# Last twenty attention steps as ten blocks of two steps with two dense groups at once, and a quotient by reciprocal on VectorE

## The chip, the cores and the metric

One core of one Trainium2 chip runs the program. The metric is device time in microseconds (us), the median of repeated executions. TensorE (PE) multiplies matrices into PSUM, which has eight banks of 128 x 512 f32; its weight loads (PEld) run beside its multiplications. ScalarE (ACT) applies functions, VectorE (DVE) and GpSimd (POOL) do elementwise work, SyncE (SP) issues the transfers. Each engine works through its own list of instructions in order.

## The reference

```python
def _A_ref(x, wq, wk, wv, wo):          # 32 heads of 16, one shared k and v
    scores = einsum("bhqd,bkd->bhqk", q, k) * (Dh ** -0.5)
    p = softmax(scores)
    return (p @ v) @ wo
def _B_ref(x, w1, b1, w2):
    h = x @ w1 + b1
    act = h * tanh(softplus(h))          # Mish
    return act @ w2
xn = layernorm(x)                        # x is 2048 x 512
s = _A_ref(xn, wq, wk, wv, wo)
g = silu(_B_ref(xn, w1, b1, w2))         # y / (1 + exp(-y))
return x + s * g
```

## The kernel before

The 2048 rows are taken in four chunks of 512 (`NC`). A unit is four heads of one chunk; there are 32 units of 16 steps, 512 steps in all (`NS`). One step takes 128 keys: four score products (`e`, L1025), each 128 keys by 512 rows for one head, an exponential of each on ACT from PSUM into an SBUF tile (`pts` or `pt`, L1030), and two steps later four value products (`pv`, L1112) that add them into one bank. The two score products of a pair stand on the two row halves of the PE array: a score needs 64 of its 128 rows, and even and odd ones alternate.

Beside the attention run the dense products in groups (`Group`): the projections, the two layers of the gate (`xps`) and the output projection (`wop`). A group adds 9 to 15 products of three-term split f32 into one bank (`Mm`). A full product uses all 128 rows (`Mm.__call__`, L112); `Mm.half` (L116) uses 64 rows and needs a second half later on the other side. Up to step 489 dense groups run as halves, on the side that the scores leave free, together with row maxima (`m`, L1054) that DVE reduces (L1058). The maxima of all units are done `LEAD` = 22 steps ahead of the end, so the last 22 steps, 490 to 511, have scores, exponentials, value products and what is left of the dense work.

These last steps are written out in the loop from L1543 on. Steps 490 and 491, and 504 to 511, are single: four scores, up to four full dense products (`fill(4)`), four value products. Steps 492 to 503 are six blocks of two steps: six scores, up to eight full dense products of one group (`fill(8)`), ACT jobs, two scores, eight value products. Scores of these steps take banks from two pools of three, `ps_e` and `ps_m` (L1015); a score waits until the exponential that read the bank before has ended.

The second gate layer of the last chunk leaves one sum `y` (128 x 512) for each of four row tiles `tt`. Its third group adds its product to `y` on DVE (L847); `s1` takes exp(-y) on ACT and limits it on POOL (L855, L179), `s2` takes Ln(e + 1) (L860), `s3` Exp of minus that (L865) and POOL multiplies (L169): y / (1 + exp(-y)). In the same way `n0` and `n1` (L1136, L1140) take the softmax sum of unit 30 to its reciprocal in `sc`, and `n2` makes the output tile `ot_all` on POOL. ACT jobs stand in a queue that the loop empties at marked places (`act_jobs`).

The output projection of the last chunk is split (`wo_groups`): nine of twelve products of each row tile run before the last unit ends, each in a bank of its own (`alloc`), the last three after it. The first group of tiles 0, 1, 2, 3 may start from step 496, 504, 507 and 512 on.

Of the kernel before, what the change touches and what calls it, by code (L numbers as in the profile page):

```python
# [39 lines left out]
HALF = P // 2  # L40
HOLD = 1
STEP_US = 2.88
K_US = {0: 2.7, 6: 2.86, 7: 3.07, 8: 3.07}
UNIT_US = 11.75
XMAX = 8
NPT = 14
# [76 lines left out]
def block_kernel(ctx: ExitStack, tc: tile.TileContext, x, wq, wk, wv, wo, w1, b1, w2, out):  # L123
# [53 lines left out]
    def pool_min(o, lim):  # L177
        charge(0.7)
        pool.tensor_scalar(o, o, lim, 0.0, op0=ALU.min, op1=ALU.max)  # L179
# [216 lines left out]
    def later(k, fn):  # L396
        at(step[0] + k, fn)
# [3 lines left out]
    def job(fn, free=None):  # L401

        jobs.append((fn, free))
# [184 lines left out]
    def chunk_size(n):  # L588
        return -(-n // -(-n // XMAX)) if n else 0
# [238 lines left out]
    def m2_groups(c, third, its, m1s):  # L828
        lo, hi = THIRDS[third]

        def ready(tt):
            done = m1_done.get((c, hi - 1))
            return None if done is None else done - g_of[tt].most

        g_of = []

        def mk(tt):
            def post(ps):
                if tt == 3:
# [7 lines left out]
                dve.tensor_tensor(out=y, in0=ps, in1=y, op=ALU.add)  # L847
                if third < 2:
                    return
                st = {}  # L850

                def s1():
                    e = st["e"] = sb.tile([P, D], F32, tag="t", name=f"e{c}_{tt}", bufs=2)
                    st["free"] = hold(t_hist)
                    act.activation(e, y, AF.Exp, scale=-1.0)  # L855
                    pool_min(e, EMAX)
                    at(pool_at(0.3), lambda: job(s2))

                def s2():
                    act.activation(st["e"], st["e"], AF.Ln, bias=one)  # L860
                    job(s3)

                def s3():
                    e = st["e"]
                    act.activation(e, e, AF.Exp, scale=-1.0)  # L865
                    mul(pool, y, y, e)
                    y_done[c, tt] = pool_at(0.2)
                    st["free"]()
                later(0.5, lambda: job(s1, t_free))

            g = Group(mm12(lambda j, a: act_of[c, lo + j][:, a, P * tt:P * (tt + 1)],
                           lambda j, b: its[j].tile[:, b], hi - lo), post, its, [lambda: ready(tt)])
            g.dve = third > 0
            g.late = 3 if hi - lo == 5 else 2
            g_of.append(g)
            return g
        return [mk(tt) for tt in range(4)]
# [6 lines left out]
    def wo_groups(c):  # L884
        last = c == NC - 1
        its = [item("wb", ("o", k), wo[P * k:P * (k + 1), :]) for k in range(4)]
        first, second = [], []
        adds = []

        def mk(tt):  # L890
            st = {}
            t = 4 * c + tt

            def pre():
                if xr_hist[-4] is None:
                    return False
                st["x"] = sb.tile([P, D], F32, tag="xr", name=f"xr{t}", bufs=4)
                st["free"] = hold(xr_hist)
                sp_at(0.5)
                sp.dma_start(st["x"], xr[t])  # L900
                return True

            def store():
                sp.dma_start(outr[t], st["x"])
                st["free"]()

            def post(ps):
# [12 lines left out]
                at(step[0] if last else pool_at(0.1), store)  # L920

            mms = mm12(lambda j, a: ot_of[c, j][:, a, P * tt:P * (tt + 1)],
                       lambda j, b: its[j].tile[:, b], 4)
            done = [lambda: ot_done.get((c, 3)), lambda: y_done.get((c, tt))]
            if not last:
                first.append(Group(mms, post, its, done, pre, wo=c))
                first[-1].dve = True
                return
            kept = {}

            def alloc():
                pool_, tag = ((ps_x, "x"), (ps_m, "m"), (ps_m, "m"), (ps_e, "e"))[tt]
                kept["ps"] = pool_.tile([P, D], F32, tag=tag, name=f"wop{tt}")
                return kept["ps"]
            first.append(Group(mms[:9], lambda ps: None, its, [lambda: NS - (16, 8, 5, 0)[tt], lambda: ot_done.get((c, 2))], wo=c, alloc=alloc))
# [72 lines left out]
    def e_one(s, i):  # L1008

        v, r = divmod(s, 16)  # L1010
        if s < NS - LEAD:
            a, k, p = 1 - s % 2, r - r % 2 + i // 2, i % 2
        else:
            a, k, p = i % 2, r, i // 2
        ps, tag = (ps_m, "m") if NS - LEAD <= s and i in ((1, 3) if s < NS - 8 else (3,)) else (ps_e, "e")  # L1015
        pt = None
        if i > 1 and s % 4 == 1 and PAIRS[0] < s < PAIRS[1]:
            pt = sb.tile([P, C], F32, tag=("qh", "ql")[i - 2], name=f"pt{s}_{i}", bufs=1)
        return score(v, a, k, p, ps, tag, pt)()

# [93 lines left out]
    def o_out(v):  # L1114
        c, g = divmod(v, 8)
        b, k = divmod(g, 2)
        os_ = sb.tile([P, C], F32, tag="os", name=f"os{v}", bufs=1)
        if v == NU - 1:
            o_last(os_)
            return  # L1120
        act.activation(os_, pv_of[v], AF.Copy)
        if k == 0:
            o_of[0] = sb.tile([P, C], F32, tag="oc", name=f"oc{v}", bufs=1)
            o_of[1] = sb.tile([P, C], F32, tag="sc", name=f"sc{v}", bufs=1)
        oc, sc = o_of[0], o_of[1]
        for e, t in ((16, sc), (0, oc)):
            for j in range(4):
                r = 64 * k + 16 * j
                sp_at(0.63)
                sp.dma_start(t[r:r + 16], os_[32 * j + e:32 * j + e + 16])  # L1130
        rows = slice(0, HALF if v == NU - 2 else P)
        if v == NU - 2:
            turn_rows()
        if k == 1 or v == NU - 2:
            def n0():
                act.activation(sc[rows], sc[rows], AF.Ln)  # L1136
                job(n1)

            def n1():
                act.activation(sc[rows], sc[rows], AF.Exp, scale=-1.0)  # L1140
                later(0.5, n2)

            def n2():
                if b == 0 and c > 0 and wo_left[c - 1]:
                    later(0.5, n2)
                    return
                ot = ot_of[c, b] = ot_all[:, b]
                mul(pool, oc[rows], oc[rows], sc[rows])
                hi_pool(ot[rows, 0], oc[rows])
                sub(pool, ot[rows, 1], oc[rows], f(ot[rows, 0]))  # L1150
                if k == 1:
                    ot_done[c, b] = pool_at(0.2)
            later(3, lambda: job(n0))

    turn_of = {}

# [335 lines left out]
    def unit_ready(s):  # L1492
# [7 lines left out]
            g.most = 2  # L1500
        return ok and 12 < len(cur["g"].mms) <= len(UNIT) - 1

    for s in range(NS + 2000):
        inm = s < NS - LEAD
        if s < skip[0]:
# [87 lines left out]
```

## Time and profile before

| | |
|---|---|
| median of 3 runs | 1575.98 us (1575.85 to 1577.67) |
| the profiled execution, its time | 1576.23 us |
| the profiled execution, span of its instructions | 1574.5 us |
| PE busy over the span | 1559.7 us, 99% |
| ACT, DVE, POOL busy | 1295.0, 1333.2, 636.8 us |
| scores of step 490 start | 1503.09 us |
| scores of step 510 start | 1555.57 us |
| last value product ends, output projection's last products follow | 1561.43 us |

Times inside the profile are counted from the span's start. The busy shares are averages over the whole span; the change touches the last 72 us alone, where DVE has next to nothing to do. A PE instruction's time in the profile overlaps its neighbours' on the other row half or column group, so lengths of stretches are read from start to start.

### The profile page before, as it was taken

How to read it: one execution, taken by the hardware profiler on the slowest of the kernel's cores; microseconds unless marked ns; L12 is line 12 of the kernel's file. 1: busy time of each engine (PE TensorE's matmuls, PEld its weight loads, DVE VectorE, ACT ScalarE, POOL GpSimd, SP SyncE). 2: the span in 40 equal slices, each digit the busy share in tenths (PEclk: the TensorE clock that was granted, in tenths of full speed). 3: DMA queues.
4: the chain of work that ended last, by engine and by line, in shares of the span. 5: the costliest groups of instructions: out<-in, count | busy, mean ns of one | idle time of the engine just before them, and what ended most of it. 6: DMA issues, size and time to landing. Idle time of an engine off the chain costs nothing.

```text
span 1574.5 us, 31330 instructions
## 1 busy us (share of the span) xinstructions
PE 1559.7 (99%) x11681; PEld 876.0 (56%) x11681; DVE 1333.2 (85%) x2275; ACT 1295.0 (82%) x2509; POOL 636.8 (40%) x672
## 2 busy tenths in 40 slices
PE   9999999999999999999999999999999999999998
PEld 6555655655555565565555556556555555655643
DVE  7998888888989988888898988888889898888821
ACT  6489888789898778977989788897888978888796
POOL 4787348356356203321615422162153423215021
PEclk9999999999999999999999999999999999999999
DMA  6243134133141303212123230322322213031200
GB/s 206 88 138 105 46 97 149 32 112 118 45 157 51 106 16 111 72 32 93 50 69 98 91 92 21 103 64 83 97 58 78 76 46 113 15 98 32 75 21 27
DMA packets 74119, 125.21 MB, mean 80 GB/s; under 512 B 21536, under 2 KB 35648, under 8 KB 73968
## 3 DMA queue, kind: packets, MB, share of 16 engines
q1 hardware_dynamic: 73968, 123.21, 25.2%
q8 instruction: 93, 1.52, 0.4%
q14 instruction: 58, 0.48, 0.1%
HBM read 75.31 MB, written 26.21 MB: 64 GB/s over the span
## 4 chain that ended last, share of the span: by engine, by line
PE 96%; ACT 2%; DVE 1%; DMA 0%; POOL 0%; issue 0%; DVEq 0%; POOLq 0%; ACTq 0%
PE xps L116 43%; PE pv L1112 31%; PE m L1054 11%; PE e L1025 6%; PE xps L112 2%; ACT pts L1030 1%; DVE mb L1058 1%; PE warm L1269 1%; PE kp L335 0%; PE wop L112 0%; PE xp L294 0%; PE warm L1348 0%; DMA rawwb<-in_dram 0%; DMA ks<-ks 0%; ACT hb L778 0%
## 5 line engine op out<-in xcount | busy, mean ns | idle before, releaser
L1058 DVE TENSOR_REDUCE mb<-m 128x1 f32<-128x512 f32 x2048 | 1265.7, 682 | 169.6 <-PE m L1054 121.6
L1030 ACT ACTIVATE pts<-e 128x512 f32<-128x512 f32 x2042 | 1062.8, 607 | 220.6 <-PE e L1025 157.1
L1054 PE MATMUL m<-ks,qt 48*128 48x512 f32 (+1 forms) x2048 | 841.5, 425 | 1.2 <-DMA ks<-ks 0.7
L1025 PE MATMUL e<-qt,ks 64*128 64x512 f32 x2048 | 748.0, 407 | 1.8 <-ACT pts L1030 1.7
L1112 PE MATMUL pv<-pts,vaug 128*32 128x512 f32 x4084 | 531.0, 603 | 0.0
L1054 PEld LDWEIGHTS m<-ks,qt 48*128 48x128 f32 (+1 forms) x2048 | 367.3, 185 | 106.7 <-DVE mb L1058 53.2
L1025 PEld LDWEIGHTS e<-qt,ks 64*128 64x128 f32 x2048 | 372.3, 186 | 28.6 <-ACT pts L1030 19.1
L116 PE MATMUL xps<-wbs,act 64*128 64x512 f32 x1248 | 315.2, 397 | 0.0
L116 PE MATMUL xps<-xt,ws 64*128 64x512 f32 x1128 | 313.3, 410 | 0.3 <-ACT pts L1030 0.3
L116 PEld LDWEIGHTS xps<-xt,ws 64*128 64x128 f32 x1128 | 194.5, 185 | 183.4 <-ACT pts L1030 121.4
L116 PEld LDWEIGHTS xps<-wbs,act 64*128 64x128 f32 x1248 | 225.9, 185 | 66.4 <-ACT pts L1030 32.7
L1112 PEld LDWEIGHTS pv<-pts,vaug 128*32 128x32 f32 x4084 | 87.8, 108 | 151.1 <-issue 143.1
L169 POOL TENSOR_TENSOR hb<-hb,t 128x512 f32<-128x512 f32 x56 | 72.2, 1289 | 161.6 <-ACT t L797 81.3
L179 POOL TENSOR_SCALAR t<-t 128x512 f32<-128x512 f32 x56 | 34.4, 614 | 180.1 <-ACT t L784 180.0
L116 PE MATMUL xps<-xt,wq 64*128 64x512 f32 x336 | 93.0, 409 | 0.0
L116 PEld LDWEIGHTS xps<-xt,wq 64*128 64x128 f32 x336 | 57.9, 185 | 55.2 <-ACT pts L1030 37.7
L116 PE MATMUL xps<-wbs,ot_all 64*128 64x512 f32 x288 | 79.3, 408 | 0.0
L169 POOL TENSOR_TENSOR oc<-oc,sc 128x512 f32<-128x512 f32 (+1 forms) x16 | 20.6, 1290 | 144.8 <-DMA wbs<-w 71.3
L116 PEld LDWEIGHTS xps<-wbs,ot_all 64*128 64x128 f32 x288 | 49.5, 184 | 46.9 <-ACT pts L1030 28.5
L169 POOL TENSOR_TENSOR act<-hb,act 128x512 fp32r<-128x512 f32 x56 | 72.2, 1289 | 4.7
L169 POOL TENSOR_TENSOR hb<-hb,u 128x512 f32<-128x512 f32 x56 | 72.2, 1290 | 4.4
L169 POOL TENSOR_TENSOR u<-u,t 128x512 f32<-128x512 f32 x56 | 71.9, 1284 | 4.7
(146 smaller groups left out, 872.0 us busy)
## 6 DMA issues: line engine op xcount, KB each, us to landing
wbs<-w SPq DMA_DIRECT2D x38, 512.0 KB
ws<-w SPq DMA_DIRECT2D x35, 512.0 KB
qt<-qh SPq DMA_DIRECT2D x256, 32.0 KB
w<-wbs SPq DMA_DIRECT2D x14, 512.0 KB
wq<-wq SPq DMA_DIRECT2D x14, 512.0 KB
wbs<-wo SPq DMA_DIRECT2D x12, 512.0 KB
w<-ws SPq DMA_DIRECT2D x11, 512.0 KB
rawws<-in_dram SPq DMA_DIRECT2D x21, 256.0 KB
```

Of the source, the lines that this page charges most:

```text
L112: self.pe.matmul(ps, self.lhs(), self.rhs(), start=(self.k == 0), stop=(self.k == self.tot - 1))
L116: i = self.pe.matmul(ps, self.lhs()[o], self.rhs()[o], start=(self.k == 0 and self.halves == 0), stop=(self.k == self.tot - 1 and self.hal ...
L169: eng.tensor_tensor(out=o, in0=a, in1=b, op=op)
L179: pool.tensor_scalar(o, o, lim, 0.0, op0=ALU.min, op1=ALU.max)
L1025: pe.matmul(e, ks[o:o + 64, P * k:P * (k + 1)], q[o:o + 64, p], start=True, stop=True)
L1030: x = act.activation(dst, e, AF.Exp, scale=0.25)
L1054: pe.matmul(m, q[o, p, P * t:P * (t + 1)], ks[o, C * kb:C * (kb + 1)], start=True, stop=True)
L1058: return dve.reduce_max(out=mb_of[v][:, kb, z:z + 1], in_=m, axis=AX.X)
L1112: pe.matmul(o[32 * j:32 * j + 32], vaug[:, k], pt, start=(k == 0), stop=(k == 15))
L1269: pe.matmul(warm, qts[0][:, 0, 0:P], qts[0][:, 0], start=True, stop=True)
```

## The change

The region of two-step blocks now reaches from step 490 to step 509: ten blocks (`PAIRS`). A block (`tail_block`) issues the four scores of its first step, then the dense work, then the four scores of its second step, then eight value products. Its dense work comes from two groups at once (`lanes`): a chunk of up to eight products of each, as halves, one group on row half 0 and the other on row half 1, issued in turn. In the next block the same two chunks run again on the other halves. The third group of row tile 2 takes a bank of `ps_m` (`y2ps`), and all of the first three output groups may start from step 496.

For row tiles 1 to 3 of the last chunk, `s2` and `s3` are gone: POOL limits e and adds 1, and DVE takes the reciprocal and multiplies. For unit 30, `n_last` takes the reciprocal of `sc` on DVE in place of `n0` and `n1`.

```diff
-K_US = {0: 2.7, 6: 2.86, 7: 3.07, 8: 3.07}
+K_US = {-1: 2.3, 0: 2.7, 6: 2.86, 7: 3.07, 8: 3.07}
...
                     act.activation(e, y, AF.Exp, scale=-1.0)
+                    if c == NC - 1 and tt > 0:
+                        charge(0.7)
+                        pool.tensor_scalar(e, e, EMAX, 1.0, op0=ALU.min, op1=ALU.add)
+                        dve.reciprocal(e, e)
+                        ew(dve, y, y, e, ALU.mult)
+                        y_done[c, tt] = pool_at(0.2) + 2
+                        st["free"]()
+                        return
                     pool_min(e, EMAX)
...
+            if (c, third, tt) == (NC - 1, 2, 2):
+                g.alloc = lambda: ps_m.tile([P, D], F32, tag="m", name="y2ps")
...
-                pool_, tag = ((ps_x, "x"), (ps_m, "m"), (ps_m, "m"), (ps_e, "e"))[tt]
+                pool_, tag = ((ps_m, "m"), (ps_x, "x"), (ps_m, "m"), (ps_e, "e"))[tt]
...
-            first.append(Group(mms[:9], lambda ps: None, its, [lambda: NS - (16, 8, 5, 0)[tt], ...
+            first.append(Group(mms[:9], lambda ps: None, its, [lambda: NS - (16, 16, 16, 0)[tt], ...
...
-        ps, tag = (ps_m, "m") if NS - LEAD <= s and i in ((1, 3) if s < NS - 8 else (3,)) else (ps_e, "e")
+        ps, tag = (ps_m, "m") if NS - LEAD <= s and i in ((1, 3) if s < NS - 6 else (3,)) else (ps_e, "e")
         pt = None
-        if i > 1 and s % 4 == 1 and PAIRS[0] < s < PAIRS[1]:
+        if i > 1 and s % 4 == 3 and PAIRS[0] < s < PAIRS[1]:
...
-            later(3, lambda: job(n0))
+            def n_last():
+                dve.reciprocal(sc[rows], sc[rows])
+                n2()
+            if v == NU - 2:
+                later(4, n_last)
+            else:
+                later(3, lambda: job(n0))
...
-    PAIRS = NS - LEAD + 2, NS - 8
+    PAIRS = NS - LEAD, NS - 2
...
+    def tail_block(s):
...
+            side = (s // 2 + n) % 2
+            mms = ln["g"].mms
+            second = ln["chunk"] is not None
+            if not second:
+                left = len(mms) - ln["n"]
+                ln["chunk"] = mms[ln["n"]:ln["n"] + (left if s >= NS - 6 else chunk_size(left))]
+            for k, m in enumerate(ln["chunk"]):
+                def half(m=m, k=k, ln=ln, side=side, second=second):
+                    i = m.half(ln["ps"], side)
...
+                xs[side].append(half)
...
+        es = [[(s + j // 2, 2 * (j % 2) + a) for a in range(2)] for j in range(4)]
+        for j in range(2):
+            for e in es[j]:
+                e_one(*e)
+        for j in range(max(len(x) for x in xs)):
+            for x in xs:
+                if j < len(x):
+                    x[j]()
+        for ln in ends:
+            for i in ln["g"].items:
+                i.users -= 1
+            ln["g"].post(ln["ps"])
+            ln["g"].done = s
+        relay = e_one(*es[2][0])
+        for e in es[2][1:] + es[3]:
+            e_one(*e)
...
+        act_jobs(3)
+        for n in range(s - 2, s):
+            pv(n)
...
             if s % 2 == 0:
-                es = [(s + n // 4, n % 4) for n in range(8)]
-                for n in es[:6]:
-                    e_one(*n)
-                fill(8)
-                act_jobs(4)
-                for n in es[6:]:
-                    e_one(*n)
-                for n in range(s - 2, s):
-                    pv(n)
-                if s % 16 == 0:
-                    o_out(s // 16 - 1)
+                tail_block(s)
+            halves[0] = -1
```

How the lists of instructions move, at three places. Names: `e_6_0_1` is the score of step 6 of the unit, head pair 0, row half 1; the block of steps 502 and 503 has steps 6 and 7 of unit 31. `wop` are banks of the output projection, the number telling which; `wop_20934` is row tile 0 and `wop_21034` row tile 1 after the change.

PE before, the block of steps 502 and 503: six scores, one full product, two scores, the value products.

```order
L1025 MATMUL e_6_1_1_21017<-qt_78,ks 128x512
L1025 MATMUL e_7_0_0_21020<-qt_78,ks 128x512
L1025 MATMUL e_7_0_1_21023<-qt_78,ks 128x512
L112 MATMUL wop_20975<-wbs,ot_all 128x512
L1025 MATMUL e_7_1_0_21030<-qt_78,ks 128x512
L1025 MATMUL e_7_1_1_21033<-qt_78,ks 128x512
L1112 MATMUL pv_20946<-pts,vaug 32x512 x6
```

PE after, the same block: four scores, nine halves of two output groups, four scores, the value products.

```order
L1035 MATMUL e_6_0_0_21035<-qt_78,ks 128x512
L1035 MATMUL e_6_0_1_21038<-qt_78,ks 128x512
L1035 MATMUL e_6_1_0_21041<-qt_78,ks 128x512
L1035 MATMUL e_6_1_1_21044<-qt_78,ks 128x512
L116 MATMUL wop_20934<-wbs,ot_all 128x512
L116 MATMUL wop_21034<-wbs,ot_all 128x512
```

The second group of the output projection now has its first half here; before, its first full product stood in step 504. Its bank is the one of `ps_x` that row tile 3's third gate group has just left.

The sums of the gate's third group and what DVE holds around them. DVE before, its list from the last row maxima on:

```order
L847 TENSOR_TENSOR y_1_18731<-xps,y_1_18731 128x512
L1087 STREAM_TRANSPOSE cr_20801<-mp_20705 128x32
L847 TENSOR_TENSOR y_2_19039<-xps,y_2_19039 128x512
L847 TENSOR_TENSOR y_3_19200<-xps,y_3_19200 128x512
L1169 COPY os_21200<-pv_20946 128x256
```

DVE after, from the same place:

```order
L1097 STREAM_TRANSPOSE cr_20763<-mp_20705 128x32
L847 TENSOR_TENSOR y_1_18731<-xps,y_1_18731 128x512
L859 RECIPROCAL e_1_20859<-e_1_20859 128x512
L169 TENSOR_TENSOR y_1_18731<-y_1_18731,e_1_20859 128x512
L847 TENSOR_TENSOR y_2_19039<-y2ps,y_2_19039 128x512
L859 RECIPROCAL e_2_20972<-e_2_20972 128x512
L169 TENSOR_TENSOR y_2_19039<-y_2_19039,e_2_20972 128x512
L1164 RECIPROCAL sc_20920<-sc_20920 64x512
L847 TENSOR_TENSOR y_3_19200<-xps,y_3_19200 128x512
L859 RECIPROCAL e_3_21070<-e_3_21070 128x512
L169 TENSOR_TENSOR y_3_19200<-y_3_19200,e_3_21070 128x512
L1185 COPY os_21257<-pv_20977 128x256
```

Four reciprocals and three products came to DVE. The sum that empties `y2ps` (row tile 2) stands behind one reciprocal and one product, and the sum that empties row tile 3's `xps` behind two reciprocals and one product.

ACT before, in the block of steps 494 and 495:

```order
L1030 ACTIVATE pts<-e_15_0_0_20823 128x512
L1030 ACTIVATE pts<-e_15_0_1_20826 128x512
L860 ACTIVATE e_1_20782<-e_1_20782,one 128x512
L865 ACTIVATE e_1_20782<-e_1_20782 128x512
L1030 ACTIVATE pts<-e_15_1_0_20837 128x512
L1030 ACTIVATE pts<-e_15_1_1_20840 128x512
```

ACT after, at the end of the same block:

```order
L1040 ACTIVATE pts<-e_15_0_0_20845 128x512
L1040 ACTIVATE pts<-e_15_0_1_20848 128x512
L1040 ACTIVATE pt_2_20851<-e_15_1_0_20852 128x512
L1040 ACTIVATE pt_3_20855<-e_15_1_1_20856 128x512
L855 ACTIVATE e_1_20859<-y_1_18731 128x512
L1040 ACTIVATE pts<-e_0_0_0_20872 128x512
```

The two instructions between the exponentials of a step are gone for row tiles 1 to 3; what is left of the quotient on ACT stands behind the eighth exponential of a block.

More of the change, by code (lines that the diff above doesn't have):

```diff
@@ L931, in alloc @@
             def alloc():
-                pool_, tag = ((ps_x, "x"), (ps_m, "m"), (ps_m, "m"), (ps_e, "e"))[tt]
+                pool_, tag = ((ps_m, "m"), (ps_x, "x"), (ps_m, "m"), (ps_e, "e"))[tt]
                 kept["ps"] = pool_.tile([P, D], F32, tag=tag, name=f"wop{tt}")
                 return kept["ps"]
-            first.append(Group(mms[:9], lambda ps: None, its, [lambda: NS - (16, 8, 5, 0)[tt], lambda: ot_done.get((c, 2))], wo=c, alloc=alloc))
+            first.append(Group(mms[:9], lambda ps: None, its, [lambda: NS - (16, 16, 16, 0)[tt], lambda: ot_done.get((c, 2))], wo=c, alloc=alloc))
             second.append(Group(mms[9:], post, its, done, pre, wo=c, alloc=lambda: kept["ps"]))
@@ L1501, in unit_ready @@
         return ok and 12 < len(cur["g"].mms) <= len(UNIT) - 1
+    lanes = [None, None]
+    def tail_block(s):
+        if s == PAIRS[0] and cur["g"] is not None:
+            lanes[0] = {"g": cur["g"], "ps": cur["ps"], "n": cur["n"], "chunk": None}
+            cur["g"] = None
+        xs = [[], []]
+        ends = []
+        for n in range(2):
+            if lanes[n] is None and begin():
+                lanes[n] = {"g": cur["g"], "ps": cur["ps"], "n": 0, "chunk": None}
+                cur["g"] = None
+            ln = lanes[n]
+            if ln is None:
+                continue
+            side = (s // 2 + n) % 2
[7 more added lines that the diff above has]
+                    i = m.half(ln["ps"], side)
+                    if second and k == 0:
+                        tc.add_manual_dep(i.ins, ln["relay"].ins.name, mybir.DependencyInfo(
+                            mybir.DependencyClass.Sync, mybir.DependencyReason.DATA), reason="other half of the bank")
+                xs[side].append(half)
+            if second:
+                ln["n"] += len(ln["chunk"])
+                ln["chunk"] = None
+                if ln["n"] == len(mms):
+                    ends.append(ln)
+                    lanes[n] = None
+        es = [[(s + j // 2, 2 * (j % 2) + a) for a in range(2)] for j in range(4)]
[14 more added lines that the diff above has]
+            e_one(*e)
+        for ln in lanes:
+            if ln is not None:
+                ln["relay"] = relay
+        act_jobs(3)
+        for n in range(s - 2, s):
+            pv(n)
+        if s % 16 == 0:
+            o_out(s // 16 - 1)
     for s in range(NS + 2000):
```

## The prediction

> **What bounds the kernel now.** The page's chain gives PE 96% of the end, so I read its last stretch by engine (the view by stretches), then PE and ACT there in order of time.
>
> ```profile
> 1503.09:1555.57 52.48, 50.81 (x301) 20.91 (x297) 3.01 (x8) 47.41 (x94) 10.53 (x12) 1.00 0.06 16
> ```
>
> Columns: length, then busy time of PE, PEld, DVE, ACT, POOL. This stretch is steps 490 to 509, all that the change rewrites: 52.48 us, with PE and ACT both near full, DVE at 3.01 us.
>
> ```profile
> 1505.88 0.73 PE L1025 MATMUL e<-qt,ks 64*128 64x512 f32 x4
> 1506.55 0.73 PE L112 MATMUL xps<-xt,act 128*128 128x512 f32 x2
> 1507.21 1.06 PE L1112 MATMUL pv<-pts,vaug 128*32 128x512 f32 x8
> ...
> 1509.38 2.13 PE L112 MATMUL xps<-xt,act 128*128 128x512 f32 x8
> 1511.44 0.50 PE L1025 MATMUL e<-qt,ks 64*128 64x512 f32 x2
> 1511.87 1.92 PE L1112 MATMUL pv<-pts,vaug 128*32 128x512 f32 x16
> 1513.72 0.96 PE L1025 MATMUL e<-qt,ks 64*128 64x512 f32 x6
> 1514.61 1.20 PE L112 MATMUL xps<-xt,act 128*128 128x512 f32 x4
> ```
>
> Start to start, these rows give PE's prices. Two scores 0.43, four 0.67, six 0.89: 0.23 a pair plus 0.20 for a change of kind. Eight full dense products 2.06: 0.23 each plus 0.20. Value products of a step (eight rows, two to a product) 0.99, of two steps 1.85. By these the 20 steps need 48.4 us of PE: two single steps 2.79 + 2.32, blocks of 8, 4, 8, 4, 8 and 1 dense products 5.24, 4.31, 5.24, 4.31, 5.24, 3.61, and singles 4 x 2.79 + 2 x 2.09. So 4.1 us of the 52.48 is waiting, on ACT:
>
> ```profile
> 1519.10 0.98 PE L1025 MATMUL e<-qt,ks 64*128 64x512 f32 x2 [0.34 <-ACT pts L1030]
> ...
> 1528.65 0.73 PE L1025 MATMUL e<-qt,ks 64*128 64x512 f32 x4
> 1529.81 0.98 PE L1025 MATMUL e<-qt,ks 64*128 64x512 f32 x2 [0.43 <-ACT pts L1030]
> 1530.72 2.14 PE L112 MATMUL wop<-wbs,ot_all 128*128 128x512 f32 x8
> ...
> 1540.47 0.49 PE L1025 MATMUL e<-qt,ks 64*128 64x512 f32 x2 [0.90 <-ACT pts L1030]
> ```
>
> ```profile
> 1527.84 0.77 ACT L860 ACTIVATE e<-e,one 128x512 f32<-128x512 f32 x1
> 1528.64 0.63 ACT L865 ACTIVATE e<-e 128x512 f32<-128x512 f32 x1
> 1529.18 4.00 ACT L1030 ACTIVATE pts<-e 128x512 f32<-128x512 f32 x8
> ```
>
> Six scores take 2.07 here in place of 0.89, since ACT had Ln and Exp of the quotient in front of the exponentials that free the banks. The rows at 1519.10 and 1540.47 are the same wait for two other row tiles; PE gives some 1.1 us away at each of the three.
>
> **The change: the blocks.** The dense work is the same, 57 full products as 114 halves. SP's list does not change, and POOL, with three products less, is waited for by nobody here but DVE. Each half loads its own weights, 57 loads more, beside the products: PEld is busy 20.91 of the 52.48 us. Halves pair up as scores do, so a block with twelve halves is 8 + 12 = 20 half products, ten pairs, one change of kind: 2.33 + 0.20 + 1.85 = 4.4 us of PE, against a mean of 4.8 for blocks of 8 and 4 full ones. That halves and scores run at the pair's rate is seen before step 490:
>
> ```profile
> 1501.28 0.39 PE L116 MATMUL xps<-xt,act 64*128 64x512 f32 x1
> 1501.29 0.39 PE L1054 MATMUL m<-ks,qt 48*128 48x512 f32 x1
> 1501.51 0.39 PE L116 MATMUL xps<-xt,act 64*128 64x512 f32 x1
> 1501.52 0.40 PE L1025 MATMUL e<-qt,ks 64*128 64x512 f32 x1
> ```
>
> But a block does not reach 4.4. With `y2ps` or `wop` in `ps_m`, two of its banks are left for scores, so the eighth score takes the bank of the fourth and waits for its exponential:
>
> ```profile
> 1543.03 0.73 PE L1025 MATMUL e<-qt,ks 64*128 64x512 f32 x4
> 1543.69 1.20 PE L112 MATMUL wop<-wbs,ot_all 128*128 128x512 f32 x4
> ```
>
> ```profile
> 1506.87 4.98 ACT L1030 ACTIVATE pts<-e 128x512 f32<-128x512 f32 x10
> ...
> 1543.56 2.07 ACT L1030 ACTIVATE pts<-e 128x512 f32<-128x512 f32 x4 [0.71 <-PE e L1025]
> ```
>
> The first exponential starts 0.53 after the scores; ten take 4.98 and four 2.07, so each adds 0.49. So the fourth ends at 0.53 + 1.96 = 2.49, the eighth score starts 0.1 later, the value products 0.43 after that, and the block ends 1.85 later: 4.87 us. Blocks 502 and 504 (nine halves) hang on the same chain. Block 492 follows tile 0's Ln and Exp and takes 5.1. Blocks 506 and 508 have 13 halves, five of them without a partner: 4 + 9 slots of 0.23, 0.20, 1.85 = 5.1, bound by PE. Sum: 4.87 + 5.1 + 6 x 4.87 + 2 x 5.1 = 49.4, which is **3.1 us less** than 52.48. Steps 510, 511 and the end stay.
>
> **The reciprocals.** ACT loses three pairs of Ln and Exp and one of `sc`; that gain is in the 49.4 already. They go to DVE, which is idle, but in order with two sums that empty banks PE wants. No row shows a reciprocal (R below). The nearest:
>
> ```profile
> L847 DVE TENSOR_TENSOR y<-xps,y 128x512 f32<-128x512 f32 x5 | 3.4, 686 | 21.0 <-PE xps L112 21.0
> L169 DVE TENSOR_TENSOR xr<-wop,xr 128x512 f32<-128x512 f32 x2 | 1.3, 681 | 0.0
> L169 DVE TENSOR_TENSOR oc<-otop,sc 64x256 f32<-64x256 f32 x2 | 0.9, 427 | 1.9 <-PE otop L1177 1.9
> L1080 DVE TENSOR_REDUCE mp<-mp 128x16 fp32r<-128x16 f32 x1 | 0.2, 170 | 0.0
> ```
>
> Lower end: one pass as a sum or product, R = 0.69. A pass over 512 costs (681 - 427)/256 x 512 = 0.51 us, with 0.17 fixed. Upper end: the dearest row for its elements, 170 ns for 16, or 10.6 ns each: 5.4 us, about ten passes. I take R = 4.2, eight passes (0.17 + 8 x 0.51). [...]
>
> Walking the blocks (starts at 0, 4.9, 10.0, 14.9, 19.7, 24.6, 29.5 us after 1503.09) with
>
> ```profile
> 1522.28 0.69 ACT L855 ACTIVATE e<-y 128x512 f32<-128x512 f32 x1
> 1523.13 0.61 POOL L179 TENSOR_SCALAR e<-e 128x512 f32<-128x512 f32 x1 [3.22 <-ACT e L855]
> ```
>
> Row tile 1: exp(-y) starts behind eight exponentials of block 494, at 10.0 + 4.45 = 14.45; POOL 0.85 later, DVE 0.65 after that, at 15.95. Reciprocal, product (0.69) and then row tile 2's sum (0.69) end at 21.5. Its bank goes to the fourth score of step 498, wanted at 19.95: PE stands until 21.6. From there 0.23, six pairs, four scores and the value products end at 25.75, **1.2 us late** (0.45 hides in the wait for exponentials). Queued behind that score is everything on PE.
>
> Row tile 2: its exp(-y) starts at 25.75, the reciprocal at 27.25; two reciprocals, product and row tile 3's sum take 2 x 4.2 + 1.4, so `xps` is free for PE at 37.1. Block 502 starts at 30.6 and its first half of `wop` tile 1 wants that bank at 31.1: PE stands 6.0 us, of which 0.7 hides, since nine halves leave room in the block: **5.3 us late**. Row tile 3's reciprocal and the products of `sc` are wanted after step 511, 20 us later, and cost nothing.
>
> Sum: -3.1 + 1.2 + 5.3 = +3.4. The point from which it turns is R of about 3.2, six passes.
>
> **The clock after a stand of PE.** Block 502's stand is near 5.6 us without a product. The last product, and the stretches after it (the third column from the end is the granted clock):
>
> ```profile
> 1564.13 4.46 PE L112 MATMUL wop<-wbs,ot_all 128*128 128x512 f32 x18
> ```
>
> ```profile
> 1568.60:1572.80 4.20, 0.00 (x0) 0.00 (x0) 1.98 (x4) 0.00 (x0) 1.36 (x2) 1.00 0.64 241
> 1572.80:1574.50 1.70, 0.00 (x0) 0.00 (x0) 0.00 (x0) 0.00 (x0) 0.00 (x0) 0.50 0.06 21
> ```
>
> The warm-up products at the program's start, by stretch:
>
> ```profile
> 2.00:6.00 4.00, 4.00 (x10) 3.13 (x11) 1.00 0.96 271
> 6.00:10.00 4.00, 4.00 (x19) 3.32 (x18) 1.00 0.97 296
> ```
>
> 4.2 us after its last product PE's clock fell to half; and at the start ten products fit into 4 us where 19 follow. So a closed clock could run at half for up to 4 us and lose up to 2.0; at the least nothing. I take 0.7. Total +4.1 on 1575.98 (the profiled execution, 0.25 slower, moves alike): **1580.1 us**.
>
> **The rivals.**
>
> *The clock closes and stays half for the full 4 us:* +3.4 + 2.0, **1581.4**. For it: 5.6 is longer than the 4.2 that closed it, so I give it better than even of the dear case. Against: it was seen once, and the 4.2 may not count from PE's last product. [...]
>
> *The reciprocal is cheap*, R up to 1.8: both sums come in time and the 3.1 stays, **1572.9**, faster. For it: the 0.69 of every other row of this shape. Against: no other of these is a division.
>
> *Between*, R of 2 to 3.9: row tile 3's sum alone is late, by 2 x (R - 1.8): 1573.3 to 1578.
>
> *Halves of two groups do not pair*, so each takes its own 0.23: blocks of 12, 11, 9 and 13 halves 5.8, 5.5, 5.1, 6.0, in all 56.4, or +3.9 with cheap reciprocals: **1579.9**. Against: the pairs before step 490.
>
> **How the numbers follow.** Dear reciprocals 0.62 (1579.4 with an open clock, 0.26; 1580 to 1581.4 with a closed one, 0.36), cheap 0.19, between 0.14, no pairs 0.05. A measurement of this kernel tells 0.2%, 3.15 us, from no change. Slower: 0.19 of the 0.26, nearly all of the 0.36, and the 0.05: 0.59. Faster: a little over half of the cheap case, 0.11. The rest, 0.30, within. Own range of the likeliest: 1578.5 to 1583.0, the upper end from R = 5.4 (2.4 and 7.7 late, less 3.1). With the cheap case, whose end lies near 1572.7, the range is 1572.7 to 1583.0; what is left out is the cheap case's better part and a closed clock after the dearest reciprocal, 2 in 10 together.
>
> **What would show it.** Right: a reciprocal row on DVE near 4 us; an idle time of PE of some 5 us before `wop` in block 502, released by DVE; blocks of about 4.9 us elsewhere; no wait on Ln or Exp. Wrong: a reciprocal under 2 us and step 510 starting near 1552.5, or blocks well over 5 us with PE full.

## The result, and the profile after

| | before | after |
|---|---|---|
| median | 1575.98 us (5 runs, 1575.85 to 1579.79) | **1584.06 us** (5 runs, 1581.20 to 1584.82) |
| ratio, 95% interval | | 1.0039 [1.0023, 1.0055] |
| the same kernel again, beside other runs of before | 1577.88 us (30 runs) | 1583.30 us (11 runs), 1.0025 [1.0016, 1.0034] |
| profiled execution, its time and span | 1576.23, 1574.5 us | 1581.3, 1579.5 us |
| step 490 to step 510, start to start | 52.48 us | 58.29 us |
| from step 510 to the end of the span | 18.93 us | 18.85 us |

Slower by 0.25 or 0.39%, by the two ratios. In the two profiles all of it lies in the twenty steps, +5.81 us; 490 starts 0.73 earlier than before, and the end is as it was. The stretch by engine (columns as before):

```profile
1502.36:1560.65 58.29, 51.65 (x358) 25.59 (x354) 18.25 (x15) 43.90 (x86) 10.61 (x9) 0.94 0.06 15
```

ACT works 3.5 us less, DVE 15 us more, and the granted clock is no longer 1.00. The view of waits, PE's own over the stretch (total, times, longest):

```profile
PE wop L116 <- DVE y L847: 4.5, 1, 4.5
PE e L1035 <- DVE y L847: 1.3, 1, 1.3
PE e L1035 <- ACT pts L1040: 0.6, 2, 0.3
```

Two waits for a sum on DVE have taken the place of most of the waits for ACT. From the first scores of one block to those of the next: 4.93, 5.15 (block 492), 4.93, 4.93, **6.21** (498), 4.93, **12.17** (502), 4.94, 5.04, 5.06 us. PE in order of time at the two long ones:

```profile
1522.30 0.73 PE L1035 MATMUL e<-qt,ks 64*128 64x512 f32 x3
1524.36 0.49 PE L1035 MATMUL e<-qt,ks 64*128 64x512 f32 x1 [1.33 <-DVE y L847]
...
1533.44 0.73 PE L1035 MATMUL e<-qt,ks 64*128 64x512 f32 x4
1534.01 0.39 PE L116 MATMUL wop<-wbs,ot_all 64*128 64x512 f32 x1
1538.91 2.07 PE L116 MATMUL wop<-wbs,ot_all 64*128 64x512 f32 x7 [4.51 <-DVE y L847]
...
1542.19 3.49 PE L1122 MATMUL pv<-pts,vaug 128*32 128x512 f32 x16
```

The fourth score of step 498 stands for the bank of `y2ps`, the first half of `wop` tile 1 in block 502 for the bank of `xps`. The last row is the block's sixteen value products, 3.49 us in place of 1.9. DVE at the same time:

```profile
1519.56 3.35 DVE L859 RECIPROCAL e<-e 128x512 f32<-128x512 f32 x1 [9.41 <-POOL e L858]
1523.01 0.69 DVE L169 TENSOR_TENSOR y<-y,e 128x512 f32<-128x512 f32 x1
1523.62 0.68 DVE L847 TENSOR_TENSOR y<-y2ps,y 128x512 f32<-128x512 f32 x1
1530.91 3.35 DVE L859 RECIPROCAL e<-e 128x512 f32<-128x512 f32 x1 [6.61 <-POOL e L858]
1534.37 0.69 DVE L169 TENSOR_TENSOR y<-y,e 128x512 f32<-128x512 f32 x1
1534.97 3.34 DVE L1164 RECIPROCAL sc<-sc 64x512 f32<-64x512 f32 x1
1538.24 0.62 DVE L847 TENSOR_TENSOR y<-xps,y 128x512 f32<-128x512 f32 x1
```

Both sums stand behind reciprocals, each 3.35 us. What the first reciprocal of each queue waits for in turn is POOL's limit and plus 1, 1.9 us each:

```profile
1517.60 1.93 POOL L858 TENSOR_SCALAR e<-e 128x512 f32<-128x512 f32 x1 [8.05 <-ACT e L855]
...
1528.96 1.92 POOL L858 TENSOR_SCALAR e<-e 128x512 f32<-128x512 f32 x1 [8.97 <-ACT e L855]
```

The clock, by stretches of 3.41 us (first column after the length PE's busy time, third from the end the granted clock): one that holds the stand of 1.33, then three from within the stand of 4.51 on.

```profile
1521.51:1524.93 3.42, 2.09 (x17) 0.79 (x10) 2.69 (x3) 2.53 (x6) 0.00 (x0) 1.00 0.04 10
1535.17:1538.58 3.41, 0.00 (x0) 0.00 (x0) 3.41 (x2) 0.87 (x2) 0.18 (x1) 1.00 0.00 0
1538.58:1541.99 3.41, 3.08 (x12) 2.14 (x12) 0.28 (x1) 0.53 (x2) 2.96 (x3) 0.50 0.00 0
1541.99:1545.40 3.41, 3.41 (x17) 0.59 (x16) 0.00 (x0) 2.04 (x5) 1.28 (x1) 0.50 0.00 0
```

After a stretch in which PE did nothing it ran at half clock for 6.82 us, just when it had the block's rest to do. So the account of this execution: undisturbed blocks -2.7 (49.8 for 52.48), the two late sums, and the clock.

### The profile page after: what moved, and what is told of

Same layout as the page of the kernel before. It is cut to its first block, busy times and chain, and to the rows that moved or that the text cites. A ratio compares the mean times of both kernels' runs of the same rounds, so it can differ in the third digit from the quotient of the medians.

```text
span 1579.5 us, 31438 instructions
## 1 busy us (share of the span) xinstructions
PE 1560.3 (99%) x11738; PEld 882.5 (56%) x11738; DVE 1349.2 (85%) x2282; ACT 1291.0 (82%) x2501; POOL 636.9 (40%) x669
## 4 chain that ended last, share of the span: by engine, by line
PE 95%; DVE 2%; ACT 1%; POOL 0%; DMA 0%; issue 0%; DVEq 0%; POOLq 0%; ACTq 0%
PE xps L116 43%; PE pv L1122 31%; PE m L1064 11%; PE e L1035 6%; PE xps L112 1%; ACT pts L1040 1%; DVE mb L1068 1%; PE warm L1285 1%; PE kp L335 0%; DVE e L859 0%; PE wop L116 0%; PE xp L294 0%; PE warm L1364 0%; POOL e L858 0%; DMA rawwb<-in_dram 0%
```

## The experiments

Each kernel was measured beside the kernel before; "stretch" is step 490 to step 510 in its profile. A theory and a rival stood at the start: that the loss is the sums behind the reciprocals and the gain the blocks, against a loss in the blocks themselves.

**Either half of the change alone.** The blocks with Ln and Exp left on ACT:

```diff
-                    if c == NC - 1 and tt > 0:
+                    if False:
...
-            if v == NU - 2:
-                later(4, n_last)
-            else:
-                later(3, lambda: job(n0))
+            later(3, lambda: job(n0))
```

> The ten blocks stay, all four reciprocals are taken back (Ln and Exp on ACT, product on POOL). Theory (the loss is PE standing behind DVE's reciprocals, and its clock closing after the long stand): no wait of PE on a DVE sum, no fall of the clock before the end, blocks of 4.9 to 5.1 us as in the changed kernel's undisturbed ones, but some 1.8 us given back where Ln and Exp delay the next exponentials: 0.9 us less than before, about 1575. Rival (two groups on alternating halves are themselves dear, or bring the clock down): slower than before by 2 us or more.

1577.08 us, ratio 0.9999 [0.9990, 1.0007].

```profile
1505.20:1556.34 51.14, 48.83 (x358) 24.40 (x354) 3.11 (x8) 47.63 (x94) 10.52 (x12) 1.00 0.07 17
```

The stretch is 1.34 us shorter and PE waits for ACT alone, 2.1 us: the two-group blocks are not what costs. The times do not show the gain, since their interval holds no difference as well as the 0.9 us that I expected. And the four reciprocals alone, in the blocks of before (pools, first steps and loop put back):

```diff
-    PAIRS = NS - LEAD, NS - 2
+    PAIRS = NS - LEAD + 2, NS - 8
...
-                tail_block(s)
+                es = [(s + n // 4, n % 4) for n in range(8)]
+                for n in es[:6]:
+                    e_one(*n)
+                fill(8)
+                act_jobs(4)
...
```

> The old blocks and singles stay, the four reciprocals are added to them. Theory (a reciprocal of 3.35 us costs only where a sum that empties a bank PE wants stands behind it): in the old order row tile 3's sum stands ahead of the reciprocal of sc, both sums are 0.3 to 0.6 us late, PE's three waits of 1.1 us on Ln and Exp are gone: 2.4 us less than before, about 1573.6. Rival (a reciprocal on DVE costs by itself, wherever it stands): slower than before by 3 us or more.

1583.76 us, 1.0043 [1.0029, 1.0057], stretch 57.87: the gain of 2.4 that I expected did not come. The instruction that came late was another than in the changed kernel:

```profile
1525.16 1.85 PE L1033 MATMUL e<-qt,ks 64*128 64x512 f32 x6 [7.05 <-DMA qt<-cr]
```

```profile
1514.40 3.35 DVE L859 RECIPROCAL e<-e 128x512 f32<-128x512 f32 x1 [6.39 <-POOL e L858]
1517.86 0.69 DVE L169 TENSOR_TENSOR y<-y,e 128x512 f32<-128x512 f32 x1
1518.47 0.20 DVE L1095 STREAM_TRANSPOSE cr<-mp 128x32 f32<-128x32 f32 x1
```

The transposition of the last unit's row maxima stood behind the first reciprocal. The transfer that moves them into `qt` started late, and with it the first score of the last unit. The clock fell here too, from 1522.03 to 1528.85, with PE at work in 3.69 of these 6.82 us; half of that, 1.8, is an estimate of the loss. With the stand of 7.05 and the 49.01 us that the same kernel takes in a better order (below) it makes 57.9, so no room is left for a price of the reciprocals themselves. I had read the sums and not every row of DVE's list that comes after the new one.

**The order on DVE.** First only `sc` put behind row tile 3's sum (`later(k, f)` issues f k steps on):

```diff
-                later(4, n_last)
+                later(5, n_last)
```

> The changed kernel with one instruction moved: the reciprocal of sc stands behind row tile 3's sum on DVE. Theory: block 502 stands 1.7 us for the bank in place of 4.9, 0.7 of it hidden; block 498's 1.3 stays; the stand is too short to close the clock, so its 3 us and more are gone too: 0.4 us less than before, about 1575.6. Rival (the first gate reciprocals make the loss, that of sc is the smaller part): over 1580.

1575.19 us, 0.9997 [0.9987, 1.0008], stretch 51.99, 0.49 less than before: as expected. One number in one line takes 6.3 us out of the stretch, since the stand shrinks and the clock stays whole:

```profile
1535.64 1.17 PE L116 MATMUL wop<-wbs,ot_all 64*128 64x512 f32 x7 [1.34 <-DVE y L847]
```

Then the gate's reciprocals behind the sums as well:

```diff
-                        dve.reciprocal(e, e)
-                        ew(dve, y, y, e, ALU.mult)
-                        y_done[c, tt] = pool_at(0.2) + 2
-                        st["free"]()
+                        def quotient():
+                            dve.reciprocal(e, e)
+                            ew(dve, y, y, e, ALU.mult)
+                            y_done[c, tt] = pool_at(0.2) + 2
+                            st["free"]()
+                        later(2.5, quotient)
```

> The changed kernel with every reciprocal behind the next row tile's sum on DVE; no work is left out or added. Theory: no stand of PE on DVE, no fall of the clock before the end, all ten blocks at 4.9 to 5.1 us, 49.8 us for the 20 steps against 52.5: 2.7 us less than before, about 1573.3. Rival (reciprocals hurt wherever they stand, or the blocks are dear): as slow as before or slower.

1575.05 us, 0.9984 [0.9974, 0.9994]:

```profile
1504.36:1554.24 49.88, 48.20 (x359) 24.40 (x356) 18.32 (x15) 43.58 (x86) 10.63 (x9) 1.00 0.07 17
```

No wait for DVE is left; four short ones for exponentials are, 1.5 us. So the whole loss, the fall of the clock with it, came from the order of DVE's list, and with the order mended the change makes the kernel a little faster. Which half earns that? The same mended reciprocals in the blocks of before (the second kernel of this part with the last edit):

```diff
-                        dve.reciprocal(e, e)
...
+                        def quotient():
+                            dve.reciprocal(e, e)
...
+                        later(2.5, quotient)
```

> The kernel before with the four reciprocals, each behind the next row tile's sum and behind the transposition of the row maxima on DVE; the old blocks and singles stay. Theory (what PE lost before was the wait on Ln and Exp; the two-group blocks only pay when those are gone as well): no stand of PE on DVE or on a transfer, 49.2 us for steps 490 to 509, as good as the new blocks with the sums first (49.9). Rival (the gain comes from the halves in pairs): 51 us or more.

1575.06 us, 0.9980 [0.9970, 0.9989]:

```profile
1507.71:1556.72 49.01, 49.01 (x301) 20.48 (x297) 18.22 (x15) 43.10 (x86) 10.63 (x9) 1.00 0.07 17
```

PE is busy from end to end. The gain is Ln and Exp leaving ACT, 3.47 us; the two-group blocks, worth 1.34 while ACT is in the way, are 0.87 longer than the old ones once it is not, since their eighth score still waits for the fourth exponential. This rests on the stretches, which the next profiles repeat (the new blocks take 24.98 us from step 490 to step 500, where these took 24.99; the old ones 49.01 to step 510); the two ratios, 0.9984 and 0.9980, do not tell the block forms apart.

**The two prices that I had wrong.** In the mended kernel, row tile 1 with plus 1 before the limit, row tile 2 with a limit (min, then max 0) and a plus 1 (add, then times 1) apart, row tile 3's reciprocal in two halves of 256:

```diff
-                        pool.tensor_scalar(e, e, EMAX, 1.0, op0=ALU.min, op1=ALU.add)
+                        if tt == 1:
+                            pool.tensor_scalar(e, e, 1.0, EMAX, op0=ALU.add, op1=ALU.min)
+                        elif tt == 2:
+                            pool.tensor_scalar(e, e, EMAX, 0.0, op0=ALU.min, op1=ALU.max)
+                            pool.tensor_scalar(e, e, 1.0, 1.0, op0=ALU.add, op1=ALU.mult)
+                        else:
+                            pool.tensor_scalar(e, e, EMAX, 1.0, op0=ALU.min, op1=ALU.add)
...
+                            for z in ((slice(0, D),), (slice(0, D),), (slice(0, 256), slice(256, D)))[tt - 1]:
+                                dve.reciprocal(e[:, z], e[:, z])
```

> The new blocks with the sums first on DVE; GpSimd's limit and addition in three forms: addition then minimum in one instruction (row tile 1), minimum with maximum and then addition with multiplication in two (row tile 2), minimum then addition in one as in the change (row tile 3); row tile 3's reciprocal in two halves of 256 columns. Same values up to rounding. Theory (the pair minimum and addition is dear in one instruction, 1.92 us, and a reciprocal's price goes by its elements): 0.61 us twice for the two, about 1.9 for addition and minimum, 1.92 again; halves of a reciprocal near 1.75 us each. Since nobody waits on them the time is that of sums first: 1.6 permille under before. [...]

1575.36 us, 0.9982 [0.9972, 0.9992]. POOL:

```profile
1516.65 1.93 POOL L859 TENSOR_SCALAR e<-e 128x512 f32<-128x512 f32 x1 [8.04 <-ACT e L855]
...
1526.61 0.62 POOL L861 TENSOR_SCALAR e<-e 128x512 f32<-128x512 f32 x1 [7.55 <-ACT e L855]
1527.31 0.63 POOL L862 TENSOR_SCALAR e<-e 128x512 f32<-128x512 f32 x1
...
1540.06 1.94 POOL L864 TENSOR_SCALAR e<-e 128x512 f32<-128x512 f32 x1
```

One instruction with min and add costs 1.93 us in one order and 1.94 in the other, two with other pairs 1.25 together. DVE did nothing during either of the dear rows, so they did not wait for the reciprocal. And DVE:

```profile
1542.03 3.37 DVE L868 RECIPROCAL e<-e 128x256 f32<-128x256 f32 x2 [5.46 <-POOL e L864]
```

Two halves took 3.37 together where the whole took 3.35, so here the reciprocal's price goes by the column; `sc` on 64 partitions takes 3.34, as much as 128. The old blocks with the two cheap instructions:

```diff
-                        pool.tensor_scalar(e, e, EMAX, 1.0, op0=ALU.min, op1=ALU.add)
+                        pool.tensor_scalar(e, e, EMAX, 0.0, op0=ALU.min, op1=ALU.max)
+                        pool.tensor_scalar(e, e, 1.0, 1.0, op0=ALU.add, op1=ALU.mult)
```

> The old blocks with the reciprocals behind the sums (49.0 us from 490 to 510), and POOL's limit and plus 1 as two instructions of 0.62 and 0.63 in place of one of 1.92. Theory (POOL's 0.67 us is waited for only by the reciprocal, and the reciprocal by nobody soon): no change, stretch 49.0, ratio to the kernel before 0.998 as without this edit. Rival (the quotient's time still sets something late in the kernel, as the last tile's output): 0.5 us less or more.

1573.63 us, 0.9975 [0.9964, 0.9986], stretch 49.01. The interval covers the 0.9980 without the edit: no difference shown.

**The clock.** Would work for PE during the stand keep the clock whole? In the changed kernel, the third and fourth score of step 502 issued nine times each into their own banks:

```diff
-        pe.matmul(e, ks[o:o + 64, P * k:P * (k + 1)], q[o:o + 64, p], start=True, stop=True)
+        for _ in range(times):
+            pe.matmul(e, ks[o:o + 64, P * k:P * (k + 1)], q[o:o + 64, p], start=True, stop=True)
```

> The changed kernel; the third and fourth score products of step 502 are each issued nine times into the same bank (the same values, 16 extra half products of 0.23 us), so that PE works through most of its stand before the first product of the output projection's row tile 1. Theory (3 us of block 502 are the clock, closed by the stand): the granted clock stays full, the stand for DVE's sum ends at the same time, block 502 takes about 9.2 us in place of 12.2, the 20 steps 55.3 in place of 58.3. Rival (the 12.2 us are the late bank alone, or repeats on one row half do not count as work for the clock): block 502 stays at 12 us.

1582.98 us, 1.0026 [1.0016, 1.0037], block 502 10.70: missed. PE's own row, and two stretches:

```profile
1541.64 1.14 PE L116 MATMUL wop<-wbs,ot_all 64*128 64x512 f32 x6 [1.62 <-DVE y L847]
```

```profile
1538.85:1542.26 3.41, 1.79 (x13) 1.13 (x13) 2.73 (x2) 1.13 (x2) 1.14 (x1) 1.00 0.00 0
1542.26:1545.67 3.41, 3.41 (x18) 1.61 (x18) 0.00 (x0) 2.00 (x5) 2.00 (x3) 0.50 0.00 0
```

The repeats stood too early and were too few: a stand of 1.62 was left, and the clock fell after a stretch in which PE was busy for 1.79 of 3.41 us. Beside it the unchanged kernel:

> The changed kernel once more, beside the others on one chip. Theory: 1581 to 1585 us, its runs in groups 3 us apart, by whether the clock closes once more at the program's opening, which both kernels do in part of their runs; the stretch from step 490 to 510 takes 58 us whatever the opening does. Rival (the 1584 us runs stand longer in block 502): a profile of a run near 1584 shows over 60 us there.

1583.30 us, 1.0025 [1.0016, 1.0034], with the same stand (4.52) but block 502 at 10.62 in place of 12.17:

```profile
1539.55:1542.96 3.41, 0.00 (x0) 0.00 (x0) 3.41 (x2) 0.62 (x2) 0.42 (x1) 1.00 0.00 0
1542.96:1546.37 3.41, 3.32 (x16) 2.18 (x17) 0.04 (x1) 0.77 (x2) 2.72 (x3) 0.50 0.00 0
```

One stretch at half clock, where the first profile had two. The stand ends 0.33 into a half-clock stretch in the first (PE busy 3.08 of it, and another follows), 0.09 here (3.32, and the clock opens). That this makes the difference is a reading of one profile each and not shown; the program's opening, below, has half-clock stretches with PE busy throughout after which the clock stayed at half. The steps 490 to 510 take 56.66 us in this execution of 1583.76 us, and 58.29 in the first, of 1581.30, so what makes some executions 3 us longer lies elsewhere: the first has its clock whole in the opening (1.00 from 18 to 42 us), and this one's mean clock over the span is 0.996 for the first's 0.997 although it has 3.41 us less of half clock in the block. A third profile of the changed kernel, and eighteen full products in the stand:

```diff
+        for _ in range(times):
+            pe.matmul(e, ks[:, P * k:P * (k + 1)], q[:, p], start=True, stop=True)
         pe.matmul(e, ks[o:o + 64, P * k:P * (k + 1)], q[o:o + 64, p], start=True, stop=True)
```

> The changed kernel once more beside the last: block 502 with a stand of PE of 4.5 to 4.9 us and one or two windows of 3.4 us at half clock, so 10.6 or 12.2 us; stretch 490 to 510 56.7 or 58.3.

One run, 1578.57 us; stand 4.54, one stretch at half clock, block 502 10.70. Here the stretch ahead of it was not wholly idle:

```profile
1534.64:1538.05 3.41, 0.33 (x2) 0.30 (x4) 3.02 (x2) 0.18 (x1) 0.85 (x1) 1.00 0.00 0
1538.05:1541.46 3.41, 3.41 (x16) 1.86 (x16) 0.00 (x0) 1.47 (x4) 2.30 (x3) 0.50 0.00 0
```

> Ahead of the third score of step 502 eighteen full products (128 rows, keys and queries as they stand) go into the bank that this score then fills; nothing is left out and no value changes. They take 18 x 0.23 = 4.1 us and lie in the time in which PE stood for row tile 3's sum (4.5 to 4.9 us). Theory (the clock closes where PE idles, and half-array repeats, as tried before, count as too little work): the clock stays whole, PE's own stand before wop's first half falls under 1 us, block 502 takes about 9.2 us as the sum's lateness alone makes it, stretch 490 to 510 about 55.3, time about 1581 where the unchanged kernel has 1583 to 1584. Rival (the clock closes for another reason than PE's standing, or any doubling of one bank counts as idle): half clock for 3.4 or 6.8 us in the block all the same, block 502 10.6 to 12.2, stretch 56.7 to 58.3, time 1583 to 1584.

1579.15 us, 1.0018 [1.0008, 1.0029], block 502 9.14, stretch 55.22, clock whole:

```profile
1537.64 0.50 PE L1037 MATMUL e<-qt,ks 64*128 64x512 f32 x2
1538.07 4.46 PE L1036 MATMUL e<-qt,ks 128*128 128x512 f32 x18
1542.46 0.49 PE L1037 MATMUL e<-qt,ks 64*128 64x512 f32 x2
1542.80 1.51 PE L116 MATMUL wop<-wbs,ot_all 64*128 64x512 f32 x8
...
1546.78 0.50 PE L1037 MATMUL e<-qt,ks 64*128 64x512 f32 x2
```

From the first row to the last, the same late sum (in the first profile it ends 5.42 us into the block) without the clock makes a block of 9.14 us. So the stand itself costs 9.14 - 4.93 = 4.2, and the clock 3.0 in the first profile (12.17) and 1.5 in the other two (10.62, 10.70), a little under half of the 6.82 and 3.41 us. The times do not show this: the one execution of the unchanged kernel beside these took 1578.57, and the profiled one of these, at 1582.44, has a mean clock of 0.996 over the span, with 1.00 in the stretch, so it lost time elsewhere.

**The opening.** Four of the profiles so far show half clock in the program's opening too, for two or three stretches that begin between 25.75 and 27.28 us; three more have mean clocks of 0.996, too low for the half clock in their last steps alone. Just ahead PE stands for the first transfer of `ks`: 0.85, 0.94 and 0.98 us in three of the four, 0.59, 0.69 and 0.70 in three profiles whose clock stayed whole there. The stretch around that stand, in the kernel before, which stayed whole:

```profile
23.16:26.57 3.41, 2.72 (x14) 1.45 (x13) 2.18 (x4) 2.85 (x11) 1.85 (x7) 1.00 0.30 70
```

and in the old blocks with the two POOL instructions, which did not:

```profile
22.67:26.08 3.41, 2.47 (x15) 1.32 (x13) 1.82 (x4) 2.85 (x10) 1.75 (x7) 1.00 0.32 75
26.08:29.49 3.41, 3.41 (x15) 1.16 (x11) 1.61 (x3) 3.04 (x8) 0.99 (x2) 0.50 0.89 330
29.49:32.91 3.42, 3.42 (x15) 1.63 (x12) 2.04 (x4) 1.08 (x3) 0.00 (x0) 0.50 0.24 52
```

PE is busy for 2.18 to 2.57 us of that stretch in the four where the clock then fell, and for 2.71 to 2.79 in four where it did not. If that stretch decides, four products there mend it:

```diff
             d = max(T["DVE"], s + 0.45)
+            if sum(m_next) == 2:
+                for _ in range(4):
+                    pe.matmul(lead["w"], qts[2][:, 0, 0:P], qts[2][:, 0], start=True, stop=True)
```

> The last kernel (old blocks, reciprocals behind the sums, POOL's limit and plus 1 in two instructions) with four full products of the warm-up kind put into the program's opening, ahead of the third row maxima, where PE stands 0.69 to 0.94 us for the first transfer of ks. In the profiles so far the window of 3.41 us around that stand had PE busy 2.18 to 2.57 us where the clock then fell to half (four kernels) and 2.71 to 2.79 where it stayed whole (four more). Theory (that window decides the half clock in the opening, which part of the executions of every kernel show): the four products take 0.9 us, the window holds 3.2 us or more, no execution shows the opening at half clock, every span's mean granted clock is 0.998 or more, the times lie together near 1571 to 1572.5 where the last kernel's spread from 1570.9 to 1577.2, median about 1572.0, ratio to the kernel before about 0.9965 or less. Rival (the opening's half clock comes from something else, or falls a window later): mean clocks still down to 0.996 in half of the executions, median near 1573.6 and the same spread.

**1571.94 us** (1571.49 to 1574.26), 0.9967 [0.9955, 0.9979], the lowest ratio of all, though its interval overlaps the 0.9975 without the four products. None of its six spans has a mean granted clock under 0.998, where six of the ten of the kernel before beside it have 0.996 or 0.997:

```profile
23.34:26.76 3.42, 3.42 (x17) 1.80 (x15) 1.94 (x4) 2.86 (x10) 2.14 (x8) 1.00 0.39 107
26.76:30.17 3.41, 3.41 (x18) 1.44 (x19) 2.77 (x6) 2.72 (x8) 0.60 (x1) 1.00 0.83 299
```

One of the six, at 1574.26 us, lies above the 1571 to 1572.5 expected with a mean clock of 0.998; why is open. This edit has nothing to do with the change studied, and its median without the other edits was not measured.

## Why the prediction was right, and where it was not

The prediction was slower by 4.1 us, by two late sums that eat more than the blocks gain. The mechanism, both places and the sign held; the profiled execution moved by 5.1. The sizes of several terms were off, and that the sum came near is in part luck: with two stretches at half clock the measured terms make +5.8, with one +4.3.

| term | predicted | measured |
|---|---|---|
| twenty steps without the stands | -3.1 | -2.7 |
| row tile 2's sum, step 498 | +1.2 | +1.3 |
| row tile 3's sum, block 502 | +5.3 | +4.2 |
| the clock after it | +0.7 | +3.0, or +1.5 |

*What bounds the kernel.* PE, with 4.1 us given away to ACT. Held in the main: with Ln and Exp off ACT and the list of DVE in order, 3.47 come back and PE has no wait left, so PE's own work is 49.0 us and not 48.4.

*The blocks.* 4.87 and 5.1 us, measured 4.93 and 5.04 to 5.15; the chain from fourth exponential to eighth score is what bounds them. That halves of two groups pair was right. What I did not ask was what the old blocks would do with the same relief: better.

*The reciprocal.* The mis-sized step: R = 4.2 by eight passes, measured 3.35. The bounds of 0.69 and 5.4 held it, the choice between them did not. No run shows eight passes: the rows have 3.35 us, which at the 0.17 fixed and 0.51 a pass that I used would be 6.2.

*POOL's limit and plus 1.* Mis-sized the other way: I read 0.65 from the row of a limit, and min with add takes 1.92. The row of ACT that starts row tile 1's quotient:

```profile
1516.81 0.70 ACT L855 ACTIVATE e<-y 128x512 f32<-128x512 f32 x1
```

From exp(-y) to the reciprocal's end I had 0.85 + 0.65 + 4.2 = 5.7 us, and the profile has 1516.81 to 1522.91, 6.1. The two errors cancelled there. With R = 3.35 alone corrected, the sums would have come to 1.2 - 0.85 and 5.3 - 1.7, and the total without the clock to +0.9, which is within 0.2% and would have been wrong. So the right answer for step 498 rests partly on luck. The threshold "R of about 3.2" falls with it, as it holds only at POOL's 0.65; by the prediction's own sum (3.4 less three times the fall of R) it should also read 3.1, and the rival "between" should end at 3.0, where row tile 2's sum turns late as well.

*Row tile 3's sum.* Two reciprocals instead of one because `sc` came in between, as predicted; 1.7 us shorter by R, and later by POOL: +4.2 for the +5.3.

*The clock.* The step that failed most: "a closed clock could run at half for up to 4 us and lose up to 2.0", of which I took 0.7. It closed in all three profiles, with a stand of 4.5 us and not 5.6, and the first lost 3.0. No run shows the 0.7 or the 4 us: half clock lasted 6.82 us in the first profile and 3.41 in the other two. Nor did PE have to be wholly idle before it: in the third profile the clock closed after a stretch with 0.33 us of work, and beside the repeated scores after one with 1.79.

*The range.* 1572.7 to 1583.0 held the profiled 1581.3, and the ratios on 1575.98 give 1579.9 and 1582.1. The median of 1584.06 lies 1.1 above it. Its runs have mean clocks of 0.995 to 0.997, which fits the opening's half clock, about 3.4 us (an estimate: half of two stretches) in part of the executions, on top of that in block 502; the profile before showed none in the opening, and I had no term for it.

## What to carry to other kernels

Work moved to an idle engine was free here only where it stood behind every short instruction that another engine waits for (49.88 us for the twenty steps, 58.29 where it did not): list all that stands after it in that queue, a transposition that feeds a transfer as much as a sum that frees a bank. A stand of TensorE can cost more than its length: here one of 4.5 us cost 4.2, and the clock after it another 1.5 or 3.0. So a stand of a few us is worth splitting, filling or moving. Where a change pairs a relief with a new structure, measure the relief in the old structure: here it was the whole gain.

## What the runs showed of the hardware that was not expected

- VectorE's reciprocal of 512 f32 columns takes 3.35 us on 128 partitions and 3.34 on 64, five times a sum's 0.69; two of 256 take 3.37 together.
- GpSimd's two-operation instruction on 128 x 512 f32 costs 0.62 or 0.63 us with min and max or add and times, and 1.92 to 1.94 with min and add in either order.
- TensorE's clock changed on a grid of 3.41 us: in the first profile of the changed kernel it fell at 1538.58, opened at 1545.40 and fell again at 1576.12, which is 6.82 and 30.72 us apart, 2 and 9 times 3.413. In the rows shown it fell after stretches with 0.00, 0.33, 1.79 and 2.47 us of PE's busy time and not after 2.09 and 2.72. In the last steps it opened after 3.32 and 3.41 but not after 3.08; in the opening it stayed at half after 3.41. Since 2.09 (scores and halves, two at once) held and 2.47 (the opening's small products) did not, and since 3.41 opened it in one place and not in the other, PE's busy time alone does not tell when it changes; what does stays open.
